# Output projection of a second attention layer: eight block products as a task in the pipeline, or seven as a phase of their own

## The chip, the cores and the metric

The kernel runs on one core of a Trainium2 chip. The metric is device time in microseconds (us) of one launch. TensorE (PE in the profile) multiplies, VectorE (DVE) and ScalarE (ACT) do the work on vectors, GpSimd (POOL) does small arithmetic and issues some DMAs, and SyncE's queue (SP) issues most DMAs.

## The reference

Two layers with the same weights run one after the other on x, which has 2048 rows of 1024 values in bf16. Each layer is an attention block and a feed-forward block, both with a residual:

```
def _A_ref(x, wqkv, wo):          # 32 heads of 32, a window of 8 keys with a dilation of 2
    q, k, v = (x @ wqkv), split and laid out by head
    logits  = q . k at positions s, s-2, ..., s-14, times Dh**-0.5, masked where negative
    o       = softmax(logits) . v
    return o @ wo                 # the output projection
def _B_ref(x, w1, w3, w2):
    return (silu(x @ w1) * (x @ w3)) @ w2
x = x + _A_ref(layernorm(x), ...); x = x + _B_ref(layernorm(x), ...)     # layer 0
x = x + _A_ref(layernorm(x), ...); x = x + _B_ref(layernorm(x), ...)     # layer 1
```

wqkv is 1024 x 3072, wo is 1024 x 1024, w1 and w3 are 1024 x 3584, and w2 is 3584 x 1024.

## The kernel before

**Units.** The rows are cut into four chunks of 512. A unit is the feed-forward of one chunk in one layer: units 0 to 3 are the chunks of layer 0 and units 4 to 7 those of layer 1. `b_stage(u)` runs a unit in two splits, the first 16 and then the last 12 of the 28 blocks of the hidden width. Units 0 and 1 multiply plainly. From unit 2 on every feed-forward product is done by a scheme of seven block products for eight (P1 to P7, Winograd's form of Strassen's). For these, sums of the weights are made once, on ACT and DVE during units 0 and 1 and the stages before, and kept in DRAM (`t_d`, `t2_d`).

**A split from unit 2 on.** `products` first runs `pipeline` over groups of w1 and w3, whose weights arrive as tiles called `early` and `late`, and then `second`, the product with w2, whose step is `W(name, j)` for two row blocks j. In both, a product goes into a PSUM bank A, ACT copies A into a bank B (the `tB` copy), P5 goes into a bank D and is copied to a buffer `s5`, P6 accumulates onto A and is copied to a buffer `su`, DVE adds `su` to D, P7 accumulates onto A again, and DVE adds `s5` to it, into `s22`. The four results leave through DVE instructions that add them to x. In `second` the two row blocks have an `s5` each, but share one `su` and one `s22`. A product is eight 256-column matmuls in `pipeline`, and eight or six 512-column ones for each j in `second`.

**Between the units.** After units 1 to 4 come the three q, k and v projections (`q_part`) of the chunk that is three units ahead; units 5 to 7 have none. So layer 1's chunks 0 to 3 are projected after units 1 to 4.

**Attention.** It runs in halves of a chunk (256 rows) as a background of DVE work: `score_steps` and `value_steps` are generators whose instructions `background(until)` puts into gaps of the DVE plan. The result of a half is the tile `oT`, of which there are two buffers. A third half's values can't start before `o_todo` of the first is 0.

**Output projection.** `o_tile` takes 128 rows. For each half of the width it runs eight 512-column matmuls with `wo` into a bank `po` of a small PSUM pool (`side`), and DVE adds the bank to x (line 793). The tiles wait in `o_queue`, and `between` runs one of them when its `oT` is there, which happens inside the pipeline of the unit before the one that needs the chunk. After the second tile of a half, `norm_queue` gets the norm of the next unit's input. `between` passes it on unless `hold` is set (units 1 to 4, whose norms run in the q, k and v stage that follows). From unit 3 on (`on_act`) that norm is ACT work: two squares, two sums and two scalings for each half, with seven small GpSimd instructions between them, and a DMA transpose for each 128 rows. `norm_sums` then makes four sums of the transposed rows on DVE. P5 of the next unit's first group needs the first of them.

**Order.** The instructions of PE, DVE, ACT and SP are issued in the order in which the program text emits them. A planner keeps clocks (`now`) with a cost for each step, and places background work where it is planned to fit:

```
if s is None or max(now["act"], s[1]) + s[0] > now["pe"] + gate[0]:
    break
take_act(queue)
```

Weights come through a pool `wp` of six buffers in the order of a list `seq`; the next load is issued when a buffer is released.

## Time and profile before

| | before |
|---|---|
| median of 3 runs | 1532.0 us (1531.34 to 1532.1) |
| the profiled execution, its own time | 1530.2 us |
| its span in the profile | 1528.5 us |
| PE busy | 1519.7 us, 9634 matmuls |
| DVE busy | 1202.3 us, 2126 instructions |
| ACT busy | 884.7 us, 1388 instructions |
| DMA moved | 439.56 MB, mean 288 GB/s |

The profile is one execution on the chip. Its time and its span differ by 1.7 us of start and end that are not in the trace, and it lies 1.8 us under the median of the runs. Matmuls overlap, so that PE's busy time counts a matmul as longer than the room it takes: a row of sixteen 512-column matmuls takes 3.45 us, 216 ns each, although the mean of one is given as 379 ns. In the trace of before the units begin at these times: unit 2 at 555, 3 at 741, 4 at 926, 5 at 1112, 6 at 1255 and 7 at 1397 us.

### The profile page before, as it was taken

To read this page: it belongs to the slowest core of one execution; us is meant where nothing else is said; L and a number is where in the kernel's file an instruction comes from. 1 tells how busy PE (TensorE), PEld (TensorE's weight loads), DVE (VectorE), ACT (ScalarE), POOL (GpSimd) and SP (SyncE) were. 2 spreads that over 40 slices of the span, in tenths; PEclk is the share of its full clock that TensorE was granted. 3 is DMA by queue.
4 is the path that set the end of the run, shared out by engine and by line. 5 is a ranking of instruction groups with operands and counts; after the bars stand their busy time and mean duration, and the time that the engine had idled before them with its cause. 6 is when DMAs were issued, how large, how long until landed. Compare 5 with 4: busy or idle time off the path is not lost.

```text
span 1528.5 us, 25134 instructions
## 1 busy us (share of the span) xinstructions
PE 1519.7 (99%) x9634; PEld 989.3 (65%) x9634; DVE 1202.3 (79%) x2126; ACT 884.7 (58%) x1388; POOL 160.0 (10%) x308
## 2 busy tenths in 40 slices
PE   9999999999999999999999999999999999999999
PEld 7666644444444577575786767766677768686865
DVE  4788998889889898979898959798678977535445
ACT  4785476567665357455465564755557446554643
POOL 1210102121211101002001020100111001000000
PEclk9999999999999999999999999999999999999999
DMA  9777969898997888979879888898969887878885
GB/s 336 192 224 215 260 218 334 279 300 283 309 307 257 278 317 293 350 271 294 264 268 356 323 259 282 271 335 304 322 224 331 337 315 266 306 273 336 317 293 204
DMA packets 261432, 439.56 MB, mean 288 GB/s; under 512 B 73856, under 2 KB 201088, under 8 KB 245056
## 3 DMA queue, kind: packets, MB, share of 16 engines
q1 hardware_dynamic: 248464, 390.90, 77.1%
q0 software_dynamic: 12704, 46.93, 8.6%
q8 instruction: 75, 1.23, 0.3%
q14 instruction: 45, 0.37, 0.1%
q10 hardware_dynamic: 144, 0.13, 0.0%
HBM read 345.90 MB, written 67.90 MB: 271 GB/s over the span
## 4 chain that ended last, share of the span: by engine, by line
PE 94%; ACT 3%; DVE 2%; issue 1%; DMA 0%; SPq 0%; ACTq 0%; DVEq 0%
PE st L1069 31%; PE ps L853 21%; PE w L1188 15%; PE po L788 7%; PE pg L1302 6%; PE acc L1333 6%; PE pu L1311 6%; PE pq L444 1%; ACT sg L1250 1%; PE L L611 0%; ACT L639 0%; DMA wqkv<-in_A_wqkv_dram 0%; DVE hT L1159 0%; DVE tree L597 0%; ACT L1250 0%
## 5 line engine op out<-in xcount | busy, mean ns | idle before, releaser
L853 PE MATMUL ps<-xnT,wqkv 128*128 128x512 f16 (+1 forms) x1472 | 320.5, 379 | 0.0
L1069 PEld LDWEIGHTS <-early 128*128 128x128 f16 x2688 | 262.6, 98 | 40.5 <-issue 3.5
L853 PEld LDWEIGHTS <-wqkv 128*128 128x128 bf16 x1472 | 210.7, 144 | 108.0 <-issue 2.2
L1188 PE MATMUL w<-t,hT 128*128 128x512 f16 x1008 | 225.9, 379 | 1.2 <-ACT big L1208 1.1
L1069 PEld LDWEIGHTS <-late 128*128 128x128 f16 x2016 | 197.2, 98 | 28.9 <-issue 1.1
L597 DVE TENSOR_TENSOR tree<-qT,kT 128x2048 bf16<-128x2048 bf16 x128 | 156.2, 1220 | 30.3 <-DMA kT<-qkv_d 14.5
L510 DVE TENSOR_TENSOR tree<-tree 128x1024 bf16<-128x1024 bf16 x256 | 174.8, 684 | 1.0
L1069 PE MATMUL st<-xnT,late 128*128 128x256 f16 x1344 | 174.2, 273 | 0.4 <-DVE big L1106 0.2
L1069 PE MATMUL st<-big,early 128*128 128x256 f16 x1344 | 172.2, 273 | 1.5 <-ACT st L1081 1.4
L1188 PEld LDWEIGHTS <-hT 128*128 128x128 f16 x1008 | 98.3, 98 | 113.7 <-issue 2.4
L1069 PE MATMUL st<-xnT,early 128*128 128x256 f16 x1344 | 165.8, 273 | 0.0
L682 DVE TENSOR_TENSOR tree<-At,vT 128x2048 bf16<-128x2048 bf16 x128 | 156.0, 1218 | 9.3 <-DMA At<-E 8.0
L1081 ACT COPY st<-st 128x512 f32<-128x512 f32 x84 | 48.3, 575 | 125.9 <-PE st L1069 125.2
L788 PE MATMUL po<-wo,oT 128*128 128x512 bf16 x512 | 115.7, 379 | 0.0
L1311 PE MATMUL pu<-xnT,w3t 128*128 128x512 f16 x448 | 105.8, 379 | 0.0
L1302 PE MATMUL pg<-xnT,w1t 128*128 128x512 f16 x448 | 105.8, 379 | 0.0
L857 ACT CAST hT<-ps 128x512 bf16<-128x512 f32 x96 | 55.6, 585 | 86.4 <-PE ps L853 83.0
L1333 PE MATMUL acc<-w2t,hT 128*128 128x512 bf16 x448 | 98.3, 379 | 0.0
L1094 DVE TENSOR_TENSOR st<-st,big 128x512 f32<-128x512 f32 x84 | 58.3, 695 | 45.4 <-ACT big L1090 45.2
L1250 ACT ACTIVATE sg<-st,down_scale 128x512 bf16<-128x512 f32 x126 | 86.7, 688 | 11.9 <-PE st L1069 11.6
L1069 PE MATMUL st<-big,late 128*128 128x256 f16 x672 | 87.1, 273 | 0.0
L788 PEld LDWEIGHTS <-oT 128*128 128x128 bf16 x512 | 50.1, 98 | 55.7
(167 smaller groups left out, 1920.3 us busy)
## 6 DMA issues: line engine op xcount, KB each, us to landing
early<-t_d SPq DMA_DIRECT2D x84, 1024.0 KB, 6.7
late<-t_d SPq DMA_DIRECT2D x84, 768.0 KB, 6.4
t<-t_d SPq DMA_DIRECT2D x42, 1024.0 KB, 7.6
t<-t_d SPq DMA_DIRECT2D x42, 768.0 KB, 5.2
wqkv<-in_A_wqkv_dram SPq DMA_DIRECT2D x28, 1024.0 KB, 7.5
w1t<-in_B_w_dram SPq DMA_DIRECT2D x14, 1024.0 KB, 7.8
w3t<-in_B_w_dram SPq DMA_DIRECT2D x14, 1024.0 KB, 11.3
t_d<-big POOLq DMA_DIRECT2D x28, 512.0 KB, 5.5
```

The costliest lines, as they stand in the source:

```text
L510: nc.vector.tensor_tensor(b, b, buf[:, 4:8, :], op=ALU.add)
L597: V.tensor_tensor(pr, qT[:], kT[:, :, k0:k0 + TCH], op=ALU.mult)
L682: V.tensor_tensor(tm.rearrange("p w (a e) -> p w a e", a=4), At[:].rearrange("p a w e -> p w a e"), win, op=ALU.mult)
L788: nc.tensor.matmul(ps[:], lhsT=oT[:, t, j * P:(j + 1) * P], rhs=wo[:, t, hh * 512:(hh + 1) * 512], start=(t == 0), stop=(t == KT - 1))
L853: nc.tensor.matmul(ps[:], lhsT=ws[kk // KH][:, kk % KH, t::KT], rhs=xnT[:, kk, :], start=(kk == 0), stop=(kk == KT - 1))
L1069: nc.tensor.matmul(out[:, a, :], lhsT=w[:, a, blk, k, :], rhs=rhs[:, k, :], start=start and a == 0 and k == 0, stop=k == KQ - 1, skip_grou ...
L1094: nc.vector.tensor_tensor(G["D"][:], G["D"][:], su, op=ALU.add)
L1188: nc.tensor.matmul(out[:], lhsT=lhs[:, k, j * P:(j + 1) * P], rhs=w[:, k, :], start=start and k == 0, stop=k == nq - 1, skip_group_check=True)
L1250: nc.scalar.activation(sg[:], src, ACTF.Silu, scale=inv)
L1302: nc.tensor.matmul(pg[:], lhsT=w1t[:, kk, fi * P:(fi + 1) * P], rhs=xnT[:, kk, :], start=(kk == 0), stop=(kk == KT - 1))
L1311: nc.tensor.matmul(pu[:], lhsT=w3t[:, kk, fi * P:(fi + 1) * P], rhs=xnT[:, kk, :], start=(kk == 0), stop=(kk == KT - 1))
L1333: nc.tensor.matmul(acc[:], lhsT=hT[:, f, j * P:(j + 1) * P], rhs=tiles[hh][f // nq][:, f % nq, :], start=(f == 0), stop=(f == f1 - f0 - 1))
```

## The change

For layer 1 the output projection is taken out of `o_queue`. A new function `o_products(c)` does it for a whole chunk, by seven block products for eight, between the first and the second split of the unit before (units 3 to 6). It needs sums of wo, which are made on ACT and DVE in the q, k and v stage after unit 2 and written to DRAM (`to_d`). Four of the seven blocks are loaded over `wo` in unit 3 (`wo16`), and the other three come through `wp` as two tiles `to` in each of the units 3 to 6. The scales are measured in the q, k and v stage after unit 1: squares of wo and of the v part of wqkv on ACT, as a queue `lazy` with the lowest rank. The attention result of layer 1 becomes fp16, scaled by one more small DVE instruction in each half. The norm of the next unit's input is queued at the end of `o_products`. The q, k and v stage after unit 2 uses four staging slots in `hT` for eight, because the other half of `hT` holds sums of wo.

```diff
+    spare = [hT[:, 9:16, :].bitcast(FP16), big[:, 3584:7168].rearrange("p (b c) -> p b c", b=7)]
+    wo16 = wo[:].rearrange("p k d -> p (k d)").bitcast(FP16).rearrange("p (b f c) -> p b f c", b=4, f=KT // 2)
...
+            if l == 1:
+                while "at" not in got_a[2]:
+                    yield "blocked"
+                yield 0.12, got_a[2]["at"], lambda: V.tensor_scalar(rs[:], rs[:], up_a[:, 1:2], None, op0=ALU.mult)
...
+                if f0 == 0 and u + 1 < len(units) and units[u + 1][0] == 1:
+                    seq += [("to", 4, 2), ("to", 6, 1)]
...
+    def sizes_of(m, w, i0, at):
+
+        for k in range(w.shape[1]):
+            yield 1.10, at, lambda: nc.scalar.activation(junk[:, 0:D], w[:, k, :], ACTF.Square,
+                                                         accum_out=size_a[:, m, i0 + k:i0 + k + 1])
...
+    def sums_of_wo(at):
+
+        KQ = KT // 2
+        for f in range(KQ):
+            while pending[2] and pending[3]:
+                yield "blocked"
...
+            for j, (fh, hh) in ((0, (0, 0)), (2, (0, 1)), (1, (1, 0)), (5, (1, 1))):
+                yield 0.61, max(at, stored[slot]), lambda: nc.scalar.activation(
+                    b[:, j], wo[:, KQ * fh + f, hh * 512:(hh + 1) * 512], ACTF.Copy, scale=up_a[:, 0:1])
+            makes.append([sums_of_wo_block(b, f, slot, now["act"] + 0.1), None])
...
+        nc.gpsimd.dma_start(to_d[:, :, f, :], b)
...
+    def o_products(c):
...
+        def output(j, hh, src, r):
+            xs = x_sb[:, c * TPC + j, hh * 512:(hh + 1) * 512]
+            background(r + 0.8)
+            nc.vector.scalar_tensor_tensor(xs, src, down_a[:, 0:1], xs, op0=ALU.mult, op1=ALU.add)
+            dve(0.69, r)
+
+        def run(name, j, out, start, r=0.0):
+            for k in range(KQ):
+                nc.tensor.matmul(out[:], lhsT=left[name][:, k, j * P:(j + 1) * P], rhs=right[name][:, k, :],
+                                 start=start and k == 0, stop=k == KQ - 1, skip_group_check=True)
+            return pe(KQ, max(r, at.get(name, 0.0)))
+
+        h_sum("P5", s1, H21, H22, ALU.add, oT_at[1, h0 + 1] + 0.2)
+        h_sum("P7", H21, H11, H21, ALU.subtract, 0.0)
+        s5, su, s22 = [[s_.rearrange("p a t -> p (a t)") for s_ in x] for x in (snaps[0:2], snaps[2:3] * 2, snaps[3:4] * 2)]
+        for j in range(2):
+            g = G[j]
+            g["A"] = bank("oA")
+            g["1"] = r = run("P1", j, g["A"], True)
+            g["B"] = bank("oB")
+            nc.scalar.copy(g["B"][:], g["A"][:])
+            g["tB"] = act(0.5, r)
+        h_sum("P6", H11, s1, H11, ALU.subtract, G[1]["1"])
...
+        for j in range(2):
+            g = G[j]
+            r = run("P6", j, g["A"], False, g["tB"])
+            nc.scalar.copy(su[j], g["A"][:])
+            g["tU"] = t = act(0.5, r)
+            background(t + 0.8)
+            nc.vector.tensor_tensor(g["D"][:], g["D"][:], su[j], op=ALU.add)
+            g["tD"] = dve(0.68, max(t, g["t5"])) + 0.1
...
+        for j in range(2):
+            g = G[j]
+            r = run("P7", j, g["A"], False, g["tU"])
+            background(r + 0.8)
+            nc.vector.tensor_tensor(s22[j], g["A"][:], s5[j], op=ALU.add)
+            g["tC"] = dve(0.68, r) + 0.1
+            output(2 + j, 1, s22[j], g["tC"])
...
+        for h in range(h0, h0 + R):
+            o_todo[1, h] = 0
+            norm_queue.append((key, c, (h % R,)))
+        sum_queue.append(key)
+        flush()
+        pe_requests()
...
+            if (u, f0, i) == (3, 0, 2):
+                nc.sync.dma_start(wo16, to_d[:, 0:4])
+                dma(2048)
...
                 products(u, f0, f1, hold)
+                if f0 == 0 and u + 1 < len(units) and units[u + 1][0] == 1:
+                    o_products(units[u + 1][1])
...
-            o_queue += [(l2, c2 * TPC + j) for j in range(TPC)]
+            if l2 == 0:
+                o_queue += [(l2, c2 * TPC + j) for j in range(TPC)]
...
-                q_part(*units[q], which, [weight("qkv"), weight("qkv")])
+                ws = [weight("qkv"), weight("qkv")]
+                if u == 1 and which == 0:
+                    lazy.append([sizes_of(0, wo, 0, 0.0), None])
+                if u == 1 and which == 2:
+                    lazy.extend([sizes_of(1, ws[i], KH * i, w_at[used[0] - 2 + i]), None] for i in range(2))
+                if u == 2 and which == 0:
+                    reads.append([sums_of_wo(now["pe"]), None])
+                q_part(*units[q], which, ws, (), 4 if u == 2 else 8)
+                while which == 2 and head(lazy) is not None:
+                    take_act(lazy)
                 release(2)
+            if u == 2:
+                finish_sums(lambda: "wo" in made)
+                force(makes, lambda: not any(pending))
```

## The prediction, made before the result was known

> **What bounds the kernel now.** I read the busy times first, then the chain of waits, then PE's own waits.
>
> ```profile
> PE 1519.7 (99%) x9634; PEld 989.3 (65%) x9634; DVE 1202.3 (79%) x2126; ACT 884.7 (58%) x1388; POOL 160.0 (10%) x308
> ...
> PE 94%; ACT 3%; DVE 2%; issue 1%; DMA 0%; SPq 0%; ACTq 0%; DVEq 0%
> ```
>
> PE is the chain. Its waits in the feed-forward phases add up to under 3 us, the largest in the w2 products being this (total, times, longest):
>
> ```profile
> PE w L1188 <- ACT big L1208: 1.1, 3, 0.5
> ```
>
> So a matmul less is time less, and any new wait of PE is time more. How much the others have left is read by stage (time, then the busy time of PE, PEld, DVE, ACT, POOL): the q, k, v stages after units 1 and 2, unit 5 (first pipeline, first w2 product, second split), and unit 6's second split:
>
> ```profile
> 513.00:555.00 42.00, 42.00 (x201) 27.45 (x200) 35.10 (x55) 15.16 (x25) 2.19 (x4) 1.00 1.01 336
> 699.00:741.00 42.00, 42.00 (x198) 27.59 (x197) 35.19 (x62) 23.56 (x37) 10.92 (x15) 1.00 0.94 279
> 1112.00:1179.00 67.00, 66.59 (x532) 51.52 (x531) 57.69 (x99) 49.12 (x78) 9.92 (x18) 1.00 0.84 272
> 1179.00:1200.00 21.00, 21.00 (x101) 9.63 (x99) 20.76 (x33) 3.03 (x5) 0.00 (x0) 1.00 1.02 387
> 1200.00:1255.00 55.00, 54.80 (x421) 40.64 (x420) 45.98 (x80) 30.67 (x48) 2.26 (x4) 1.00 0.83 292
> 1342.00:1397.00 55.00, 55.00 (x423) 41.16 (x421) 28.41 (x46) 28.06 (x45) 0.00 (x0) 1.00 0.78 276
> ```
>
> DVE is nearly full until unit 6. The first pipeline holds four `o_tile`s (13.8 us of 67); without them its ACT work stands in a shorter time.
>
> **What the Trainium skill says.** "TensorE: Matmul & The Clock Gate" (Back-to-back issue gap) gives 518 cycles for an isolated 512-column matmul, 216 ns at 2.4 GHz, but 131 ns sustained. This trace shows 216 (16 in 3.45 us), which I use. "VectorE: DVE Perf Modes" (perf-mode tier table) has tensor_tensor with a PSUM operand at 1x and 16-bit SBUF at 2x: the rows below agree, 695 ns for 512 columns from PSUM against 692 for 1024 in fp16. "ScalarE: Activation LUTs" (What ACT_TABLE_LOAD costs) adds 93 ns for a pointer scale: 711 ns in the row L1026 against 575 to 595 without.
>
> ```profile
> L788 PE MATMUL po<-wo,oT 128*128 128x512 bf16 x512 | 115.7, 379 | 0.0
> L1173 DVE SCALAR_TENSOR_TENSOR x_sb<-w,down,x_sb 128x512 bf16<-128x512 f32 x72 | 52.7, 745 | 9.7 <-PE w L1188 9.3
> L1211 DVE TENSOR_TENSOR w<-w,big 128x512 f32<-128x512 f32 x24 | 16.7, 695 | 14.6 <-ACT big L1208 14.3
> L1159 DVE TENSOR_TENSOR hT<-hT 128x1024 f16<-128x1024 f16 x18 | 12.5, 692 | 0.6
> L1208 ACT COPY big<-w 128x512 f32<-128x512 f32 x24 | 14.1, 586 | 20.2 <-PE w L1188 10.2 <-DVE w L1211 9.7
> L318 ACT ACTIVATE xn<-x_sb 128x1024 f16<-128x1024 bf16 x64 | 68.0, 1063 | 0.4
> L345 ACT ACTIVATE xn<-x_sb,mom 128x1024 f16<-128x1024 bf16 x32 | 39.3, 1242 | 16.3 <-POOL mom L328 16.3
> ```
>
> **The change, part by part.**
>
> *Matmuls.* Layer 1 has 4 chunks x 4 row blocks x 2 halves x 8 = 256 projection matmuls; after, 4 x 7 x 2 x 4 = 224. 32 x 0.216 = **-6.9 us**. (Two size products add 0.1.) A chunk takes 13.8 us of PE before, 56 x 0.216 = 12.1 after.
>
> *Waits inside the new phase.* Before, nothing waited for a `po` bank. The new chain has the shape of the w2 product's, seen here in unit 3:
>
> ```profile
> 816.71 0.59 ACT L1208 COPY big<-w 128x512 f32<-128x512 f32 x1
> ...
> 818.46 0.69 DVE L1211 TENSOR_TENSOR w<-w,big 128x512 f32<-128x512 f32 x1
> ...
> 819.24 0.59 ACT L1208 COPY big<-w 128x512 f32<-128x512 f32 x1 [0.90 <-DVE w L1211]
> 819.86 0.70 DVE L1211 TENSOR_TENSOR w<-w,big 128x512 f32<-128x512 f32 x1
> ```
>
> The second copy needs `su` read by the first add. There PE has two steps of 1.73 us before P7 of j = 1; here two of 0.86. From the end of P6 (j = 0): 0.1 + 0.59 (copy) + 0.05 + 0.70 (add) + 0.1 + 0.59 = 2.1 us against 1.73, so 0.4 us of wait even with an idle DVE. Behind P7 on PE stands everything else. And DVE isn't idle: until `s22` of j = 1 is made, which P4 (j = 1) needs, it has, at the spacing of neighbours in the trace (0.6 to 0.75), the last w2 output 0.7, four sums of oT 2.7, two outputs 1.4, two adds 1.35, s22, output and s22 2.1: 8.3 us. In the built order background attention stands between these: 3.6 us in units 3 and 5, 3.0 in unit 4, by rows like L510 (684 ns) and L597 (1220 ns); none in unit 6. For unit 3, in us from the phase's start, DVE ends: w2 output 1.5 (a product stands ahead of it), three sums 3.6, a fold 3.8, output 4.5, sum 5.1, output 5.8, a fold and a product 7.6, the add 8.3. Its copy was there at 6.7, so DVE is late; the second copy ends at 8.95, and P7 (j = 1), due at 7.8, starts at 9.0. Then add 9.7, s22 10.3, two folds 11.1, output 11.75, s22 12.5; P4 (j = 1) starts at 12.55 and ends at 13.4. The same count gives 13.2 in unit 4, 13.4 in unit 5 and 12.5 in unit 6. Banks come free in the order of their release, so the next pipeline starts on early ones; its P5 waits 0.2 for the output from D in units 3 and 5. Over 4 x 12.1 that is 4.1, and with the two waits of P5 **+4.5 us** (ends: 4 x 0.4 = 1.6, and 9 if attention delays each as much again).
>
> *Late release.* oT's buffers and the banks: values of the next chunk wait for `o_todo`, now half a unit later, and are due half a unit later; both scores of that chunk can run ahead, and two values of some 22 us of DVE have 130 us: 0. If that cover were gone, PE would wait at the start of a phase.
>
> *Squares after unit 1.* 16 x (1063 + 197 - 110 overlap, 1.15) = 18 us of ACT, in a stage with 15 of 42 busy. Hidden, but the last eight alternate with copies, 0.58 + 1.15 = 1.73 for each 1.73 of PE, and the last stands ahead of unit 2's first `tB` copy, for which P6 waits: **+0.7** (0 to 2). They also hold two `wp` buffers; their next tiles are due some 10 us later: 0.
>
> *Sums of wo after unit 2.* ACT 16 x 0.71 = 11.4 on 23.6 of 42, DVE 16 x 0.42 = 6.7 on 35.2 of 42, of which much is deferrable attention; in the built order the last sum stands 11 us ahead of the end, so four POOL DMAs of 0.9 MB (row of that size: 6.4 us) have read `big` before unit 3 writes it: 0 (to 1.5). On POOL's queue they take 0.9 us each (row L1035) ahead of the At DMAs, which wait for DVE anyhow. In the first 30 us ACT has about 31 us, but six banks buffer 1.73 us each.
>
> *DMA.* 3.7 MB written, 2.1 MB of `wo16` in unit 3's pipeline, 4 x 1.5 MB of `to`: 11.8 MB on 440. The w2 stages moved 387 GB/s without a wait of PE; `wo16` is 5 us at that rate on SP's queue ahead of weight loads which stand up to six tiles early: 0 (to 2). The loads `to` pass through `wp` in the 12 us that need nothing else.
>
> *Denser pipelines.* Units 3 to 6 lose the 13.8 us in which ACT caught up. A group has 4.2 us of ACT (three copies 0.58 to 0.67, three or four activations 0.69) in 6.05 of PE. In units 3 and 4 the eight groups keep 34, half of the norm for q, k and v 7, and two exps with their table loads 6: 47 in 53 us. In units 5 and 6 the norm, 8 x 1.15 + 4 x 1.24 = 14 us, moves into the second split, whose pipeline has 25 of its own in 36. The planner counts 0.5 for a copy that takes 0.58, so ACT runs late: **+1** for all (0 to 4).
>
> *Norm of unit 6's input.* It now starts after the phase, 55 us ahead of its use, for 130. In the built order unit 5's last scaling stands in the w2 product behind an exp with its table load (1.28 us), and the four row sums stand behind its last output. From the end of unit 5 on PE: two outputs 1.5, first sum 0.7, so P5, due at 0.9, starts at 2.3 to 2.7: **+1.8** (0.5 to 6: the transpose takes 4.6 us to land, up to 10). The exp between the two `su` copies adds **+0.4** (0 to 1). In unit 6 the sums stand 5 us ahead: 0.
>
> *Small.* Eight scalings of rs, scale products: under 2 us of DVE in 1200, no one waits.
>
> Sum: -6.8 + 4.5 + 0.7 + 1 + 1.8 + 0.4 = **+1.6 us** on the profiled execution's 1530.2, which stands 1.8 under the median of 1532.0. On the median: 1533.6.
>
> **The rivals.**
> *A, given back (likeliest):* as summed, within 0.2% (3.1 us, about what a measurement of this kernel can tell).
> *B, kept:* DVE takes its attention elsewhere, each phase loses 0.4, the borders 0.5 and the pipelines nothing: -6.8 + 1.6 + 0.5 = -4.7, 1527.3. For it: PE's waits before are under 3 us in a kernel as crowded as this. Against: 0.86 us a step.
> *C, slower by the late norm:* in unit 5 ACT is the bound. If its backlog of 2 us and a transpose of 10 us make the first row sum 5 us later, PE stands still, since nothing else is queued ahead of P5: 1532.0 + 1.6 + 5 + 2 = 1540.6. It decides from the point where the sum comes later than 0.9 us into unit 6; by the order it does, by how much is open. Against: earlier transposes landed in 4.6.
> *D, slower by DVE:* it enters each of the first three phases late and loses 2 us more in each: 1532.0 + 1.6 + 6 = 1539.6. DVE at 20.8 of 21 us in the w2 product before unit 5's phase speaks for it; against it, that DVE caught up before P4 in each w2 product of the trace.
> That the matmuls are not fewer is excluded: the built order has 224.
>
> **The numbers.** A 0.45, B 0.15, C 0.25, D 0.15. Faster 0.15, same 0.45, slower 0.40. Predicted 1533.6; range 1528.5 to 1541, from near B to just beyond C (A's own: 1529 to 1535).
>
> **What would show it.** 224 matmuls of oA, oB, oD; waits of P7 for the second `su` copy (over 0.3 us, four times) and of P4 for `s22` in units 3 to 5; a wait of P5 for a row sum at the start of unit 6, and of P6 for ACT at unit 2's. I am wrong if PE's waits in the phases add up to under 1.5 us or over 9, or if PE waits for DMA.

## The result: slower by 1.6%

The changed kernel takes 1555.7 us (median of 4 runs, 1552.1 to 1559.4) against 1531.7 for the kernel before beside it (4 runs): a ratio of 1.0157, 95% interval 1.0131 to 1.0183. The prediction of 1533.6 and its range to 1541 are missed. The profiled execution is the slowest of the four (1559.39 us, span 1557.7), 29.2 us longer in span than the one of before.

The page of the changed kernel, busy times and the head of the chain:

```profile
PE 1521.0 (98%) x9606; PEld 989.4 (64%) x9606; DVE 1231.4 (79%) x2194; ACT 922.8 (59%) x1460; POOL 158.0 (10%) x312
...
PE 85%; DVE 9%; ACT 3%; DMA 2%; issue 1%; SPq 0%; ACTq 0%; DVEq 0%
```

DVE's share of the chain went from 2% to 9% and DMA's from 0 to 2%, although DVE's busy share is the same: PE now waits for DVE, and DVE for DMA. Where, PE's waits tell (total, times, longest):

```profile
PE L L617 <- DVE psm L520: 14.8, 1, 14.8
PE st L1124 <- DVE big L304: 7.1, 1, 7.1
PE oA L1229 <- ACT big L1261: 4.0, 4, 1.7
PE st L1124 <- ACT sg L1400: 2.3, 2, 1.1
PE st L1124 <- ACT st L1136: 1.3, 3, 0.5
```

Two waits that happen once each make 22 us. The third line is the new phase. From the first product of each stage in the traces, where the time went (`e_two` is a version built from the results, below):

| stretch | before, us | after | e_two | after - before |
|---|---|---|---|---|
| to the start of unit 2 | 555.0 | 556.2 | 555.7 | +1.2 |
| unit 2, first pipeline | 59.9 | 61.2 | 61.3 | +1.3 |
| rest of unit 2 | 84.1 | 84.2 | 84.1 | +0.1 |
| q, k, v after unit 2 | 41.9 | 57.0 | 41.9 | **+15.1** |
| unit 3, first pipeline and w2 product, with a projection | 87.7 | 90.9 | 87.4 | +3.2 |
| rest of unit 3 and its q, k, v | 97.2 | 98.9 | 97.1 | +1.7 |
| unit 4 and its q, k, v | 185.9 | 184.3 | 184.1 | -1.6 |
| unit 5 | 143.5 | 143.1 | 145.2 | -0.4 |
| unit 6 | 141.7 | 150.4 | 141.8 | **+8.7** |
| unit 7 | 131.6 | 131.5 | 131.7 | -0.1 |

**Unit 3's start.** Timelines of PE and of DVE (start, busy us, line; in brackets the idle time before):

```profile
741.71 1.46 PE L869 MATMUL ps<-xnT,wqkv 128*128 128x512 f16 x6
758.01 0.62 PE L617 MATMUL L<-psm,gather 128*32 128x512 bf16 x4 [14.85 <-DVE psm L520]
758.57 1.89 PE L1124 MATMUL st<-xnT,early 128*128 128x256 f16 x8
```

```profile
734.75 0.42 DVE L1067 TENSOR_TENSOR big<-big 128x512 f16<-128x512 f16 x1
751.36 0.69 DVE L304 TENSOR_TENSOR big<-xnT 128x1024 f16<-128x1024 f16 x1 [16.18 <-DMA xnT<-xn]
...
757.67 0.29 DVE L520 TENSOR_TENSOR psm<-tree 128x256 bf16<-128x256 bf16 x1
```

DVE stands 16 us at the first row sum of unit 3's input (L304), which waits for a transpose. Behind it in DVE's order are folds of attention scores (L520), for one of which a small product of PE (L617) waits, and that product stands ahead of unit 3's P1. The reader sees a chain of three in-order queues: DMA holds DVE, DVE holds PE. SP's queue, which issues the transposes (start, issue time):

```profile
727.59 4.09 SPq L353 DMA_TRANSPOSE xnT<-xn  x1
731.77 0.54 SPq L880 DMA_DIRECT2D qkv_d<-hT  x1
732.41 6.75 SPq L353 DMA_TRANSPOSE xnT<-xn  x1
```

and the issues of 727 to 733 us (KB each, median us to landing), then those of the same two transposes in the kernel before (724 to 728 us):

```profile
to_d<-hT POOLq DMA_DIRECT2D x1, 896.0 KB, 12.6
qkv_d<-hT SPq DMA_DIRECT2D x1, 256.0 KB, 15.1
xnT<-xn SPq DMA_TRANSPOSE x2, 18.3
```

```profile
qkv_d<-hT SPq DMA_DIRECT2D x2, 256.0 KB, 2.5
xnT<-xn SPq DMA_TRANSPOSE x2, 3.1
```

A transpose took 3.1 us before and 18.3 now; a write of the sums of wo went out beside it, 0.7 us later. After the idle time PE is also slower (window, length, PE busy and count; the clock is the third value from the end, DMA share and GB/s follow):

```profile
743.20:758.00 14.80, 0.00 (x0) 0.00 (x0) 6.47 (x12) 2.15 (x4) 0.00 (x0) 0.61 0.89 235
746.50:758.00 11.50, 0.00 (x0) 0.00 (x0) 6.47 (x12) 2.15 (x4) 0.00 (x0) 0.50 0.84 265
758.00:763.50 5.50, 5.49 (x28) 3.61 (x28) 1.39 (x2) 1.17 (x2) 0.00 (x0) 0.50 1.01 292
763.60:814.70 51.10, 49.96 (x442) 43.05 (x440) 43.19 (x75) 40.16 (x64) 5.44 (x11) 1.00 0.95 346
```

The Trainium skill, "TensorE: Matmul & The Clock Gate" (What's actually happening), has the clock fall to half after an idle window of some 3.4 us and rise again after as much work. The trace agrees in kind: the clock is 0.50 from 3.3 us after the last product on, and for the first 5.5 us of work (not 3.4), in which eight half-width products take 1.89 us for 1.04 later. The first pipeline takes 56.1 us where before, without its 13.8 of projection, it took 53.2. 5.5 us at half the clock do 2.75 us of work, so by this estimate the clock makes nearly all of the 2.9.

**Unit 6's start.** SP's queue again:

```profile
1266.32 2.71 SPq L353 DMA_TRANSPOSE xnT<-xn  x1
1269.13 1.19 SPq L751 DMA_DIRECT2D late<-t_d  x1
1273.21 0.34 SPq L1326 DMA_DIRECT2D out_dram<-x_sb  x1
1273.65 1.91 SPq L353 DMA_TRANSPOSE xnT<-xn  x1
```

ACT had the last row block scaled at 1270.4, but an output store stands ahead of its transpose on SP and waits for DVE's output of unit 5 until 1273.2. The transpose then takes 9.5 us, beside the four broadcasts of At and the stores; the row sum starts at 1283.2 and P5 waits:

```profile
1275.80 1.04 PE L1124 MATMUL st<-xnT,early 128*128 128x256 f16 x8
1283.91 3.57 PE L1124 MATMUL st<-big,early 128*128 128x256 f16 x16 [7.07 <-DVE big L304]
```

Here too the clock is at half for the first 5.3 us of work:

```profile
1283.90:1289.20 5.30, 5.29 (x26) 3.76 (x26) 2.98 (x5) 1.18 (x2) 0.00 (x0) 0.50 1.02 407
```

The pipeline is 9.8 us longer: 7.1 of waiting and 2.7 behind it.

### The profile page after: what moved, and what is told of

It reads as the page before. It is cut to its first block, busy times and chain, and to the rows that moved or that the text cites. A ratio compares the mean times of both kernels' runs of the same rounds, so it can differ in the third digit from the quotient of the medians.

```text
span 1557.7 us, 25276 instructions
## 1 busy us (share of the span) xinstructions
PE 1521.0 (98%) x9606; PEld 989.4 (64%) x9606; DVE 1231.4 (79%) x2194; ACT 922.8 (59%) x1460; POOL 158.0 (10%) x312
## 4 chain that ended last, share of the span: by engine, by line
PE 85%; DVE 9%; ACT 3%; DMA 2%; issue 1%; SPq 0%; ACTq 0%; DVEq 0%
PE st L1124 29%; PE ps L869 20%; PE w L1338 11%; PE pg L1460 6%; PE acc L1491 6%; PE pu L1469 6%; PE po L804 4%; DMA xnT<-xn 2%; DVE tree L603 1%; DVE x_sb L1323 1%; DVE tree L516 1%; PE pq L450 1%; PE oA L1229 1%; DVE hT L1309 1%; ACT sg L1400 1%
## 5 line engine op out<-in xcount | busy, mean ns | idle before, releaser
L1124 PE MATMUL st<-big,early 128*128 128x256 f16 x1344 | 175.7, 276 | 10.7 <-DVE big L304 7.1
L603 DVE TENSOR_TENSOR tree<-qT,kT 128x2048 bf16<-128x2048 bf16 x128 | 156.1, 1219 | 18.9 <-DMA qT<-qkv_d 13.9
L1149 DVE TENSOR_TENSOR st<-st,big 128x512 f32<-128x512 f32 x84 | 58.3, 694 | 59.9 <-ACT big L1145 59.7
L518 DVE TENSOR_TENSOR tree<-tree 128x512 bf16<-128x512 bf16 x192 | 80.0, 417 | 0.0
L1491 PEld LDWEIGHTS <-hT 128*128 128x128 bf16 x448 | 43.7, 98 | 53.2 <-issue 0.8
```

The lines of the kernel that those rows point to most:

```text
L518: nc.vector.tensor_tensor(b[:, 0:2, :], b[:, 0:2, :], b[:, 2:4, :], op=ALU.add)
L603: V.tensor_tensor(pr, qT[:], kT[:, :, k0:k0 + TCH], op=ALU.mult)
L1124: nc.tensor.matmul(out[:, a, :], lhsT=w[:, a, blk, k, :], rhs=rhs[:, k, :], start=start and a == 0 and k == 0, stop=k == KQ - 1, skip_grou ...
L1491: nc.tensor.matmul(acc[:], lhsT=hT[:, f, j * P:(j + 1) * P], rhs=tiles[hh][f // nq][:, f % nq, :], start=(f == 0), stop=(f == f1 - f0 - 1))
```

## The experiments

Theory T: the POOL writes of `to_d` beside the transposes stretch both; the row sums come late, DVE and then PE stand still, and the clock falls. Rivals: R1, four staging slots for eight; R2, the ACT and DVE work of squares and sums; R3, the new phase and the pipelines around it. Each run is compared with the kernel before on the same chip (medians of 1530.6 to 1531.4 us; 1531.7 beside the changed one).

| kernel | us | ratio to before, 95% |
|---|---|---|
| changed | 1555.7 | 1.0157 (1.0131 to 1.0183) |
| e_prep: preparation only | 1549.9 | 1.0121 (1.0097 to 1.0144) |
| e_nowrite: that without writes | 1536.2 | 1.0034 (1.0021 to 1.0047) |
| e_ring: before, four slots | 1530.5 | 1.0000 (0.9991 to 1.0009) |
| e_writes: before, four writes | 1536.2 | 1.0035 (1.0022 to 1.0048) |
| e_wring: both of these | 1537.5 | 1.0042 (1.0029 to 1.0056) |
| e_wtime: e_writes, third write earlier | 1534.3 | 1.0025 (1.0015 to 1.0034) |
| e_nwrite: e_nowrite with POOL writes of wo | 1540.9 | 1.0066 (1.0049 to 1.0083) |
| e_nwsp: the same from SP | 1537.1 | 1.0047 (1.0032 to 1.0062) |
| e_sp: changed, writes from SP | 1547.1 | 1.0104 (1.0089 to 1.0119) |
| e_late: changed, last two blocks late | 1539.8 | 1.0055 (1.0040 to 1.0070) |
| e_late2: other buffers | 1539.1 | 1.0054 (1.0041 to 1.0066) |
| e_lsu: and two su buffers | 1535.8 | 1.0034 (1.0021 to 1.0046) |
| e_fix: and earlier squares | 1541.0 | 1.0064 (1.0052 to 1.0077) |
| e_front: changed, unit 5's phase first | 1549.4 | 1.0127 (1.0102 to 1.0152) |
| e_store: changed, stores later | 1545.6 | 1.0098 (1.0084 to 1.0112) |
| e_early: sums after unit 1 | 1692.0 | 1.1045 (1.1027 to 1.1064) |
| e_two | 1531.8 | 1.0006 (0.9998 to 1.0014) |
| e_twos: and stores later | 1531.1 | 1.0003 (0.9995 to 1.0011) |

### Preparation or phase?

> The changed kernel's preparation alone: the squares of wo and Wv after unit 1, the sums of wo with their four POOL writes and the ring of four staging slots after unit 2; layer 1 is projected as before, by o_tile with plain wo. Theory T (the software-queue writes stretch the DMA transposes, DVE's row sums come late, PE stands still at unit 3's start and its clock is lowered afterwards): PE idle 10 to 17 us at unit 3's start, time 1545 to 1556, without any of the new phase. Rival R3 (the phase and the denser pipelines are what costs): 1531 to 1534, PE idle under 2 us at unit 3's start.

```diff
-            if l2 == 0:
+            if l2 >= 0:
                 o_queue += ...
...
-                if f0 == 0 and u + 1 < len(units) and units[u + 1][0] == 1:
-                    o_products(units[u + 1][1])
```

1549.9: 19 of the 24 us are there without the new phase, so R3 falls as the main cause. Its four runs reach from 1544.0 to 1553.2, and the profiled one is the fastest; the loss differs from execution to execution. In it PE stands still for 4.9 us, and not for the 10 to 17 of the forecast:

```profile
739.82 2.97 PE L863 MATMUL ps<-xnT,wqkv 128*128 128x512 f16 x13
747.64 0.62 PE L617 MATMUL L<-psm,gather 128*32 128x512 bf16 x4 [4.85 <-DVE psm L520]
```

> The kernel of e_prep (preparation of the changed kernel, projection as before, 1549.9 us) with one thing left out: the four sums of wo are made by ACT and DVE but not written to DRAM (nobody reads them there). Theory T (the writes are the cause): 1531 to 1535, PE idle under 2 us at unit 3's start, the last two transposes in 3 to 6 us. Rival R2 (the sums' ACT and DVE work, the squares and the four slots delay the norm and PE by themselves): 1540 to 1550, the transposes issued later than in the kernel before or DVE's row sums late without a long landing.

```diff
-        nc.gpsimd.dma_start(to_d[:, :, f, :], b)
```

1536.2, and PE goes straight on:

```profile
737.82 4.26 PE L863 MATMUL ps<-xnT,wqkv 128*128 128x512 f16 x19
742.02 0.40 PE L617 MATMUL L<-psm,gather 128*32 128x512 bf16 x4
```

That lies just outside theory T's forecast (to 1535). Against before on its own chip the preparation costs 19.2 us with the write and 4.9 without, so that one line is worth 14.3. R2 keeps the 4.9: 1.4 in unit 2's first pipeline and waits of 1.1 to 1.7 later.

### Which property of the writes?

> The kernel before with only one edit: four staging slots instead of eight for q, k and v after unit 2. Theory T: the slots only hand the delay on; with no software-queue writes about, transposes land in 3 to 6 us and the time is 1531 to 1533. Rival R1 (a short ring blocks ACT's copies, and PE and the transposes behind them): over 1540, with ACT's copies waiting for the stores of qkv_d.

```diff
-            i = i % (7 if l == 0 else 8) * SG
+            i = i % (7 if l == 0 else ring) * SG
...
-                q_part(*units[q], which, [weight("qkv"), weight("qkv")])
+                q_part(*units[q], which, [weight("qkv"), weight("qkv")], (), 4 if u == 2 else 8)
```

> The kernel before with only the four POOL writes of 0.9 MB added after unit 2, at the points where the changed kernel has them (14, 17.5, 28 and 35 us into the stage), reading wo itself; no sums, eight slots, old projection. Theory T: the last two transposes take 10 to 19 us to land, PE idles 7 to 15 us at unit 3's start, time 1540 to 1555. Rivals R1 (ring) and R2 (ACT and DVE work of the sums): transposes in 3 to 6 us, time 1531 to 1533.

```diff
+                nc.gpsimd.tensor_scalar(tick[:, f:f + 1], sgt[:, 1, 0:1], 0.0, None, op0=ALU.mult)
+                nc.gpsimd.tensor_tensor(src[:, 0:1], src[:, 0:1], tick[:, f:f + 1], op=ALU.add)
+                nc.gpsimd.dma_start(to_d[:, :, f, :], src.bitcast(FP16).rearrange("p (b c) -> p b c", b=7))
```

(`src` is a half of wo, and `tick` adds nothing; it ties the write to a point of the stage.) The ring alone costs nothing: R1 falls. Writes alone cost 5.5, which fits neither forecast. Their transposes take 5.1 and 5.6 us and unit 3 starts on time; the loss takes another way:

```profile
746.48 1.23 DVE L599 TENSOR_TENSOR tree<-qT,kT 128x2048 bf16<-128x2048 bf16 x1 [3.22 <-DMA kT<-qkv_d]
757.02 1.03 PE L1071 MATMUL st<-xnT,late 128*128 128x256 f16 x8 [3.29 <-DVE big L1110]
```

A load of k lands at 746.4, 5 us later than in the kernel before. DVE waits for it, then has no gap until the add that PE waits for, 16 us into unit 3. So writes beside other transfers cost time here, but not by holding the row sums.

> The kernel of e_writes (before plus four POOL writes; 1536.2 us) with four staging slots for eight in the stage after unit 2. If slots and writes together make the difference between e_writes (+5.5) and the preparation of the changed kernel (e_prep, +19.2): 1543 to 1552. If the sums' own work on ACT and DVE, which moves the value load and the norm onto the writes, makes it: 1535 to 1538.

> The kernel of e_writes (before plus four POOL writes, 1536.2 us) with one edit: the third write goes out one group of q, k, v tiles earlier, some 25 us into the stage, where the transposes of unit 3's input are issued. If the moment of the write against the transposes decides: the last two transposes land in 8 to 18 us and the time rises to 1541 to 1550. If it needs the sums' work, which moves the value load and the norm into the same stretch: 1534 to 1538 as e_writes.

```diff
-        return ((None, None, None, write(0)), (write(1), None, None, write(2)), (None, write(3)))[which]
+        return ((None, None, None, write(0)), (write(1), None, write(2), None), (None, write(3)))[which]
```

(`e_wring` is `e_writes` with the edit of `e_ring`.) Neither adds anything that stands clear of `e_writes`. In `e_wtime` the third write went out 1.7 us behind the first transpose; the two transposes took 5.0 and 6.7. So the moment as tried here does not suffice.

> The kernel of e_nowrite (sums made but not stored, 1536.2 us) with four POOL writes of 0.9 MB read from wo itself, at about the moments of e_prep's (12, 15.5, 26 and 33 us into the stage). If sums and writes make the loss together (late value load and write in the stretch of the transposes): transposes of 8 to 16 us, 1545 to 1555. If it needs the writes to read the buffers of the sums (hT and big, which staging and the value chain use too): 1536 to 1541.

> As e_nwrite, but the four writes go out from SP's queue, the third directly behind the last transpose. If POOL's software queue is what stretches the transposes: under 1540 and transposes of 4 to 7 us. If the bytes do: 1544 to 1555.

```diff
-                nc.gpsimd.dma_start(to_d[:, :, f, :], src.bitcast(FP16).rearrange("p (b c) -> p b c", b=7))
+                nc.sync.dma_start(to_d[:, :, f, :], src.bitcast(FP16).rearrange("p (b c) -> p b c", b=7))
```

(`e_nwrite` is `e_nowrite` with the writes of `e_writes`; the diff is from it to `e_nwsp`.) `e_nwrite` takes 1540.9, at the edge of its second forecast, but with transposes of 9.3 and 6.6 us and 3.4 us of PE's idle time, nearer to the first. With the sums' work the value load of attention is issued at 722 and lands at 732 (in the kernel before 714 and 719), so that two weight loads, this load and a store are in flight when the transposes start, and the write comes on top. That makes 5 us of the 14. In `e_nwsp` they take 6.3 and 3.8 us, PE doesn't wait, and the four writes cost 1.6 us more than none (6.5 against 4.9), within the forecast for the software queue. But by its place on SP the third write follows both transposes there, so that queue and order changed together and the run does not tell which of them does it.

> The changed kernel with one edit: the four writes of the sums of wo go out from SP's queue, behind a store of q, k or v, and not from POOL's. If it is the software queue's descriptors that stretch the transposes: 1532 to 1538, transposes in 3 to 7 us. If it is the bytes that the writes move in this stretch, whoever issues them: 1548 to 1560, as the changed kernel (1555.7). The 7 us at unit 6's start stay in both.

```diff
-        nc.gpsimd.dma_start(to_d[:, :, f, :], b)
+        to_write.append((now["dve"] + 1.5, lambda: nc.sync.dma_start(to_d[:, :, f, :], b)))
...
             nc.sync.dma_start(qkv_d[l][which][:, t0:t0 + SG, c * CH:(c + 1) * CH], sgt)
+            write_to()
```

Here too SP's order puts the third write behind the last transpose. Transposes 8.3 and 5.9, PE's wait at unit 3's start 2.9 us for 14.8, but 8.4 at unit 6's. So 1547.1, outside both forecasts; it was the wrong run for its question, because the order changed with the queue.

> The changed kernel with one edit: blocks 3 and 4 of the sums of wo are begun only with the third q, k, v product of the stage, so that their writes (about 32 and 36 us into it) go out behind the last two transposes of unit 3's input (25 to 30 us into it). Theory T: the transposes land in 3 to 6 us as before, PE's 15 us at unit 3's start and the clock loss behind it go: 1533 to 1539 for 1555.7. Rival R2 or R3: over 1548.

```diff
-                if u == 2 and which == 0:
-                    reads.append([sums_of_wo(now["pe"]), None])
+                if u == 2 and which in (0, 2):
+                    reads.append([sums_of_wo(now["pe"], (0, 1) if which == 0 else (2, 3)), None])
```

1539.8, 15.9 us less than the changed kernel and just above the forecast. SP's queue:

```profile
727.92 3.90 SPq L353 DMA_TRANSPOSE xnT<-xn  x1
731.91 0.53 SPq L880 DMA_DIRECT2D qkv_d<-hT  x1
732.54 1.32 SPq L353 DMA_TRANSPOSE xnT<-xn  x1
```

The same transposes at nearly the same time land in 6.7 and 3.7 us, since the third write comes at 741. The stage takes 42.2 us for 57.0. Not all of the 15.9 is this: in `e_late` the exp no longer stands between the two scalings ahead of unit 6, and unit 6 loses 1.1 us there, not 7.1.

Together: it is the write beside the transposes, on top of a value load that the sums made late. The late load without a write leaves transposes of 6.0 and 4.0 us and no wait (`e_nowrite`), a write beside them without the late load 5.0 and 6.7 (`e_wtime`), both 9.3 and 6.6 or more. What is open: `e_prep`, the changed kernel, `e_front` and `e_store` have the same order with the write 0.7 us behind the first transpose, and their transposes take 8.8 to 18.9 us; `e_nwrite`, with its write 2.5 us behind and reading another buffer, has 6.6 to 9.3 and reproduces 5 us of the 14. Whether those 2 us, the buffer or chance makes that difference was not separated, nor POOL's queue from the bytes.

> The changed kernel with the sums of wo and their POOL writes (and the ring of four) moved from the stage after unit 2 to the stage after unit 1, and the squares of wo and Wv moved to layer 0's q, k and v stages. Theory T, with the writes ahead of or beside other transposes: unit 3's start loses its 15 us of idle time and some 8 us of lowered clock, 1555.7 - 23 = 1532 (1530 to 1537); the loss at unit 6's start, some 7 to 9 us, stays. Rival R3: stays above 1548. If the writes stretch whatever transposes they meet, part of the loss turns up at unit 2's start: 1538 to 1548.

```diff
+            if (c, which) == (1, 0):
+                lazy.extend([sizes_of(1, w_tiles[4 + i], KH * i, 0.0), None] for i in range(2))
+            if (c, which) == (2, 2):
+                lazy.append([sizes_of(0, wo, 0, 0.0), None])
...
-                if u == 2 and which == 0:
+                if u == 1 and which == 0:
                     reads.append([sums_of_wo(now["pe"]), None])
```

A miss by over 140 us, and no test of T or R3 (1692 is above R3's 1548, but for other reasons). The squares in layer 0 moved that layer's norm and, through ACT's order, the sums of w1, w3 and w2: PE waits begin at 136 us, SP's weight loads stand behind ACT's sums (18.5 us in one place), long before the stage that was to be tried.

### Unit 6's start

> The changed kernel with one edit: unit 5's phase stands at the start of unit 5 and not between its halves, so that the norm of unit 6's input has 120 us as before. If the late norm is what costs at unit 6's start (7.1 us of PE and its clock afterwards), the wait of P5 there goes: 1555.7 - 8 = 1548 (1544 to 1551); unit 3's loss stays. If it is not, 1554 to 1558.

```diff
         xnT = xnTs[("B", l, c)]
+        if u == 5:
+            o_products(units[u + 1][1])
         for (f0, f1) in fsplits:
...
-                if f0 == 0 and u + 1 < len(units) and units[u + 1][0] == 1:
+                if f0 == 0 and u in (3, 4, 6):
```

The pipeline of unit 6 falls to 52.7 us (62.2 in the changed kernel, 52.4 before without its projection): the late norm is the cause. But at the head of unit 5 the sums of oT are not ready (P5 waits 4.8 us for L1220 of this kernel), and the phase takes 19.7 us for 13.4. These two make a gain of about 3 us. The median falls by 6.3, inside the forecast, but not by this alone: the four runs are two of 1546 and two of 1553, and in the profiled one unit 3's start, which the edit leaves alone, lost 10 us less than in the changed kernel.

> The changed kernel with one edit: the eight output stores of unit 5's last chunk are issued behind unit 6's first group and not where they fall due, ahead of the last transpose on SP's in-order queue. If that queue holds the transpose back (scaled input ready at 1270.4, transpose issued at 1273.65): PE's wait at unit 6's start falls from 7.1 to 2 to 4.5 us and the time by 3 to 6 to 1550 to 1553. If the landing itself is slow beside the broadcasts of At: the wait stays at 6 to 8 and the time at 1554 to 1558.

```diff
+                if u == 5:
+                    stores.append(store)
+                else:
+                    store()
```

The transpose is issued at 1265.9, at once behind its scaling (ended 1265.85), lands in 4.8 us (the broadcasts of At begin 2.4 us behind it, where they began 0.8 us ahead), and the wait is this:

```profile
PE st L1124 <- DVE big L304: 1.2, 1, 1.2
```

So the stores on SP's queue made most of it: 3.3 us of delay, and with it a place behind the broadcasts, where the landing took twice as long. The exp still stands between the scalings, so it was not what cost. Unit 6's first pipeline takes 53.8 us for 62.2. The time falls by 10.1 where 3 to 6 were forecast: the clock that no longer falls was not counted, and in the profiled execution 3.4 us come from unit 3's start, which differs from run to run.

### The phase, and what is left

> The kernel of e_late (blocks 3 and 4 of the sums of wo begun only with the third q, k, v product; 1539.8 us) with the two buffers of the last pair exchanged: block 3 in big, block 4 in hT, so that the last write no longer reads the part of big that unit 3's first copy of D (s5) overwrites. In e_late that copy stands behind a write issued at 744.0 and landed at 752.4 while unit 3 began at 744.1, and PE waits 3.1 + 1.8 us. If those waits are this buffer: 1539.8 - 4.5 = 1535.3 (1533.5 to 1537). If ACT is late in unit 3 by its own work (denser pipelines): 1539 to 1541.

```diff
...
-            slot = min((i for i in (2, 3) if not pending[i]), key=lambda i: stored[i])
+            slot = (2, 3, 3, 2)[f]
```

The two waits stay (1.8 and 3.0 us; the second is now for DVE's add, L1149 of this kernel), so it was not the buffer. That ACT and DVE enter unit 3 late by the sums in the stage's last third is likely, but no run shows it.

> The kernel of e_late2 with one more edit: in the new phase each of the two row blocks has its own buffer for the copy of A after P6 (su), and s22 moves to the 'tight' part of big. The prediction's step for the waits inside the phase says that P7 of the second row block waits because its copy needs the first add to have read the shared buffer: then the four waits of oA for ACT (3.4 to 4.0 us in all in the changed kernel) shrink to under 1.5 us and the time falls by 2 to 3.5 against e_late2. If the phase is held by DVE's queue instead, the waits move to DVE (P3, P4) and the time falls by under 1.

```diff
-... (snaps[0:2], snaps[2:3] * 2, snaps[3:4] * 2)
+... (snaps[0:2], snaps[2:4], [tight_f] * 2)
```

3.3 us less than `e_late2`, as forecast. The waits of oA for ACT, 3.8 us in four, are gone; what is left of them waits for DVE:

```profile
PE oA L1230 <- DVE big L1273: 1.4, 3, 1.0
```

> The kernel of e_lsu with one more edit: the eight squares of Wv stand one q, k, v product earlier in the stage after unit 1, not beside its last copies. In the changed kernel unit 2's first pipeline takes 61.2 us for 59.9 before; if the squares at the stage's end cost that, another 1.0 to 1.5 us less than e_lsu, and PE's waits at unit 2's start under 0.2 us: about 1531. If not, the same as e_lsu.

```diff
-                if u == 1 and which == 2:
-                    lazy.extend([sizes_of(1, ws[i], KH * i, w_at[used[0] - 2 + i]), None] for i in range(2))
+                if u == 1 and which == 1:
+                    lazy.extend([sizes_of(1, w_tiles[used[0] + i], KH * i, w_at[used[0] + i]), None] for i in range(2))
```

5 us more instead of 1.3 less. Unit 2's pipeline takes 61.4 us, 61.2 without the edit (its wait is elsewhere, 1.4 us for a Silu), and at unit 6's start the exp and a store stand ahead of the last transpose again: P5 waits 6.8 us. An edit 700 us earlier has moved the order that the planner chose there.

### A version from the results

> A version built from the results: blocks 1 and 2 of the sums of wo after unit 2 and blocks 3 and 4 after unit 3, each pair where its writes landed in 4.4 us; layer 1's first chunk therefore projected as before, the new phase in units 4 to 6 only, with a buffer of its own for each su copy. Theory T: unit 3 starts and runs as in the kernel before (waits under 1 us), the three phases save 0.5 to 1.7 each against before; with the squares (1.3) and unit 6 (1.3 to 9) the time is 1530.7 to 1538. If writes disturb wherever they are, PE waits over 3 us at unit 3's or unit 4's start.

```diff
-                    reads.append([sums_of_wo(now["pe"]), None])
+                if u in (2, 3) and which == 0:
+                    reads.append([sums_of_wo(now["pe"], (0, 1) if u == 2 else (2, 3)), None])
...
-            if l2 == 0:
+            if l2 == 0 or c2 == 0:
                 o_queue += ...
...
-                if f0 == 0 and u + 1 < len(units) and units[u + 1][0] == 1:
+                if f0 == 0 and u in (4, 5, 6):
                     o_products(units[u + 1][1])
```

> e_two with the edit of e_store as well. If the output stores hold back the last transpose before unit 6, PE's wait there is under 2 us and the time is that of e_two or up to 5 us less, 1530 to 1533; without that mechanism it is the same as e_two.

PE's waits of `e_two`:

```profile
PE st L1125 <- ACT st L1137: 2.3, 5, 0.6
PE st L1125 <- DVE big L305: 1.4, 1, 1.4
PE oA L1230 <- DVE big L1273: 1.3, 2, 1.0
```

1531.8 and 1531.1: the loss is gone, and no gain that these runs can tell is left (1.0003, 0.9995 to 1.0011). Two writes in a stage, ahead of the transposes, land in 4.3 to 5.4 us in both versions and hold nobody: unit 3 starts as before (41.9 us for the stage in the table). `e_two` and `e_twos` differ by 0.6 us at most, since here both transposes stand ahead of the last six stores anyhow. No version beat the kernel before.

## Why the prediction was wrong, point by point

- *Matmuls:* right. The pages show 9634 and 9606: 28 less: 32 of the projection, and 4 more for the two size products (`e_prep`, without the phase, has 9638 weight loads for 9634).
- *Waits inside the phase:* right. P7 was forecast to wait 1.2 us in unit 3 (7.8 to 9.0) and 0.4 in unit 6, where no attention stands between; the waits are 1.7, 1.0, 1.0 and 0.4, 4.0 in all and inside the stated 1.5 to 9. The wait of P4 for `s22`, also named, does not appear, nor do rival D's 2 us more for each phase. In the trace the time between a w2 product and the next pipeline grows by 14.1, 13.7, 13.4 and 12.6 us, for 13.4, 13.2, 13.4 and 12.5. `e_lsu` shows the cause that was named, the shared `su` buffer. One stays visible in unit 3:

```profile
845.02 1.02 PE L1229 MATMUL oA<-to,oT 128*128 128x512 f16 x4 [1.67 <-ACT big L1261]
```

- *Squares after unit 1:* +0.7 forecast; P6 waits 0.5 there, the pipeline is 1.3 longer. In range, but `e_fix` does not support the reason given (squares beside the last copies).
- *Late release:* 0 holds; no wait of PE stands at the start of a phase.
- ***Sums of wo after unit 2: this step failed.*** It put four writes at "0 (to 1.5)" by two tests: POOL's issue time, and whether the writes had read `big` before unit 3. It took 6.4 us of landing from a row whose fourteen writes took 4.3 to 9.6, by what else was in flight, and asked for who overwrites the source, not for who shares the engines. Against before the preparation cost 19.2 us with the writes and 4.9 without (`e_prep`, `e_nowrite`); in the trace of the changed kernel it is 14.8 us of idle time and the half clock behind it. The Trainium skill, "DMA: Bandwidth & Descriptors" (Issuing engines are not separate DMA queues), says that transfers of all issuing engines run on the same 16 and interleave; its fit (Anatomy of one DMA, 2.0 us and the bytes at 436 GB/s) gives an estimate of 4.1 us for 917,504 bytes. The first two writes, with little beside them, took 4.4 and 4.3; the third and fourth, with the transposes, 12.6 and 15.4. So in this case the fit prices only the transfer that has little beside it. (The pointer scale of the copies shows as 116 to 136 ns in the prediction's own rows, more than the 93 that it quotes; the sum used the rows and was not hurt.) The edge that mattered was in the prediction's own list, for unit 6: row sums wait for a transpose of 4.6 us, up to 10. In unit 3 they also stand ahead of attention's folds on DVE. The trace of before held the collision as well, at 504.6 us, where one such write and two transposes went out together (the pair at 313 us, with no other transfer at its start, took 3.2). That is double the landing time, though not yet 18 us:

```profile
t_d<-big POOLq DMA_DIRECT2D x1, 896.0 KB, 6.2
xnT<-xn SPq DMA_TRANSPOSE x2, 6.2
```

- *Norm of unit 6's input:* the mechanism and the place were right, the size was not: +1.8 (0.5 to 6) for a wait of 7.1 and, with the clock, 9.8 us of the first pipeline. The exp with its table load between the scalings is there as described. Left out was SP's queue: the transpose stands behind an output store that waits for DVE. With the stores moved the wait is 1.2 (`e_store`), near the forecast. Rival C put 5 + 2 on top of the 1.8, close to what came, and was taken at one in four, but its reason was ACT's backlog and not SP's order.
- *A wait has a second price:* two idle times of PE over 7 us each brought a lowered clock. Nothing in the sum stood for it; by the estimates above it is about 2.8 of the 3.2 us in unit 3's first half and 2.7 of the 9.8 in unit 6.
- *DMA, denser pipelines:* 0 (to 2) for the loads of `wo16` and `to` holds: no wait of PE names them. +1 (0 to 4) for the pipelines did not come: with the clock taken off, unit 3 is 1.7 us longer (1.1 of it a wait for ACT in its second split), unit 4 2.0 shorter, units 5 and 6 the same.
- "I am wrong if PE waits for DMA": it did, by way of DVE. The test should have read any engine ahead of PE in the chain.

So the prediction's own phase and products are right to about 1 us. In the profiled execution the two stretches behind late transposes, unit 3's start with its first half and unit 6, hold 27.0 of the 29.2 us (15.1, 3.2 and 8.7); the squares and small waits make the rest. `e_two` has three of the phases, with two `su` buffers, without the collision, and stands 1 us above before.

## What to carry to other kernels

A transfer added to a stage is priced against what is in flight there, and first against the transfer with the shortest deadline: list the landings that an in-order engine waits for in that stretch, and put bulk writes ahead of or behind them. When a step is moved later, walk each queue that it passes and ask what the instruction just ahead of it waits for; here the output stores on SP made a wait of 7.1 us out of 1.2. A change that saves 7 us in a plan this tight can be undone by where a planner then puts one exp and one store (`e_fix`), so a version is judged at every border, not only at its own place.

## Not expected of the hardware

- Two DMA transposes of 256 KB took 3.1 us each, and 17.7 and 18.9 when a write of 0.9 MB was issued 0.7 us behind the first. In 743 to 758 us the DMA engines were busy 89% and moved 235 GB/s.
- Four kernels that issue the same writes and transposes in the same order left PE idle for 14.9, 11.5, 4.9 and 4.7 us at this one place (the profiled executions of the changed kernel, `e_store`, `e_prep` and `e_front`). Four runs of `e_prep` alone spread over 9 us, those of `e_nowrite`, without the writes, over 1.
- After 14.8 us of idle time PE's clock stayed at half for 5.5 us of work, after 7.1 us for 5.3.
